# Second mixing in seven pieces of 64 keys instead of eight overlapping ones, and the next block's scores ranked ahead

## The chip, the cores and the metric

One core of one Trainium2 chip runs the whole program. Its engines are named as in the profile: PE is TensorE (matmul; PEld its weight loads), DVE VectorE, ACT ScalarE, POOL GpSimd, SP SyncE, which issues the transfers. The metric is the device time of one execution in microseconds (us); three timed runs give a median.

## The reference

```python
scores = scale * np.matmul(q, k.transpose(0, 1, 3, 2))       # 4 batches, 12 heads, 448 tokens, 64 wide
scores = np.einsum('bhij,hg->bgij', scores, w_pre)           # first mixing of the heads
scores = scores - np.max(scores, axis=-1, keepdims=True)
attn = np.exp(scores)
attn = attn / (np.sum(attn, axis=-1, keepdims=True) + 1e-09)
attn = np.einsum('bhij,hg->bgij', attn, w_post)              # second mixing
out = np.matmul(attn, v)
...
h = x @ w_in;  x = (h * np.cos(h)) @ w_out                   # 1792 tokens, 768 -> 2048 -> 768
h = np.maximum(np.maximum(x @ w1, x @ w2), x @ w3);  out = h @ w_out2
```

## The kernel before, in words

The first part of the program is attention, in float32; the rest are the two MLPs, whose products run as three matmuls of split operands (`three`, L155 to L159).

Attention goes by score blocks. `HALVES` cuts each batch's 448 rows into four blocks of 10, 12, 12 and 11 slots in some order; a slot is ten rows, as two groups `a` of five. There are 16 blocks, numbered 0 to 15 here, and 180 slots. One, or two neighbouring, blocks form a half (`halves`), ten in all, of m columns (100 to 230).

For each block and each pair of heads, `qk` (L546 to L554) makes scores of up to 120 rows by 448 keys in PSUM; there are six pairs, so six score products a block. `evac` copies each head's scores to SBUF, and `send` (L565 to L567) scatters them by DMA into a grid whose partitions are row times head, so that mixing over heads becomes a contraction over partitions. There are two grids; block n writes the one that block n - 2 used, and may do so when that block's last first mixing is done.

A visit takes two slots of a grid. `mix1` (L569 to L577) is the first mixing, `rowmax` and `soft` the maximum and the exponentials, `wscale` puts the reciprocal sums into the second mixing's weights. `mix2` (L607 to L618) is the second mixing: per slot and row group the exponentials of 64 keys are the weights, and 60 columns (five rows, twelve heads) stream. The 448 keys are four groups `j` of 112 (`JB, JC = 4, 112`), each as two pieces of 64 that overlap by 16, one in PSUM's partitions 0 to 63 and one in 64 to 127:

```python
o = j * JC + c * (JC - 64)
nc.tensor.matmul(live["a", v, y][64 * c:64 * c + 64, j, :, a, :], live["e", v, a][k, o:o + 64],
                 live["w2s", v][k, a], start=True, stop=True)
```

`keep` (L620 to L626) copies the 480 columns of a slot from PSUM into `a2`. The 16 rows that stand twice meet zero rows of the value tiles: `vget` (L534 to L538) loads 56 rows into partitions 0 to 55 and 56 into 72 to 127. When a half is kept, `av` (L632 to L641) multiplies it by the values, two head pairs at a time, three times a half: per pair four groups `j` by two heads, 128 partitions by m columns. `keepx` and `out` write the result to DRAM as xT.

PSUM has two banks for `mix2` and `av` together (`ps_t`), two for `qk` (`ps_x`) and four for `mix1` (`ps_m`).

The order of all engines' work is made by a planner (`Plan`, L373 to L442). Each step has a rank, a cost per engine, what it follows, the ring places it takes and the steps that free them. At each point the planner takes, of the steps that could start soon on an engine, the one of lowest rank, and advances its clock by the given cost; the instructions are then written in that order, and each engine takes its own in order. Ranks count half visits: visit y has rank 2y for `mix1`, 2y + 1.5 for `mix2`. The score products of block n have rank `first[n - 1] + 0.5 + 0.125 * slots * hp`, so they spread over the visits of block n - 1 (L684).

Near the end of attention the first weights of the MLP are loaded and split, x of the first batch is loaded (`xget`, L140) and cut into two parts (L144 on ACT, L148 on DVE or POOL), and the first hidden products (`hidden`, L157 to L159) stand between the last visits.

Of the kernel before, what the change touches and what calls it, by code (L numbers as in the profile page):

```python
# [9 lines left out]
F32 = mybir.dt.float32  # L10
# [12 lines left out]
JB, JC = 4, 112  # L23
# [421 lines left out]
def attention(ctx, tc, q, k, v, w_pre, w_post, same_row, xT, tp, mlps):  # L445
# [24 lines left out]
    places = [vp.tile([128, JB, 2, D], F32, name=f"v{x}") for x in range(BUFS["v"])]  # L470
# [11 lines left out]
    for b, sizes in enumerate(HALVES):  # L482
        i = 0
        for n, half in enumerate(sizes):
            start, column, nhalf = min(i, S - RI * half[0]), 0, len(halves)
            for slots in half:
                i = min(i, S - RI * slots)
                score.append((b, i, RI * slots, slots, nhalf, column))
                column += RI * slots
                i += RI * slots  # L490
            halves.append((b, start, i - start, column, range(len(score) - len(half), len(score))))
# [42 lines left out]
    def vget(b, hp, eng):  # L534
        live["v", b, hp] = places[(b * H // 2 + hp) % len(places)]
        for a in range(2):
            to, of = a * (128 - JC // 2), a * JC // 2
            queue_of[eng].dma_start(live["v", b, hp][to:to + JC // 2], v[b, hp][of:of + JC // 2])  # L538


    def score_bank(n, hp):
        grid = lambda: ps_t.tile([128, JB, H, RI], F32, name="aps").rearrange("p j g i -> p (j g i)")[:, :S]
# [76 lines left out]

    def keep(v, y, eng):  # L620
        n, t, _ = visits[v]
        half, o = score[n][4], score[n][5] + RI * (t + y)
        if ("a2", half) not in live:
            live["a2", half] = ap_.tile([128, JB, H, NHALF], F32, name="a2")
        copy(eng, live["a2", half][:, :, :, o:o + RI].rearrange("p j g i -> p (j g) i"),
             live["a", v, y][:].rearrange("p j g a r -> p (j g) (a r)"))  # L626
# [5 lines left out]
    def av(half, x, _):  # L632
        b, _, _, m, _ = halves[half]
        a2 = live["a2", half]
        both = ps_t.tile([128, JB * H * RI], F32, name="aps")
# [588 lines left out]
```

## Time and profile before

| what | value |
|---|---|
| timed runs | 1157.16, 1154.21, 1155.92 us; median 1155.92 |
| profiled execution | 1158.33 us, span 1156.5 us |
| granted TensorE clock, mean | 0.992 |
| PE busy | 1124.7 us (97%) |
| DVE, ACT, POOL busy | 979.4 (85%), 667.0 (58%), 76.0 us (7%) |
| longest groups on PE | L157, L158, L159: 300.5, 299.8 and 299.3 us and three more; L617 (`mix2`) 119.9 us |

The span is what the profiler saw from the first to the last instruction of one execution; the execution's own time lies 1.83 us above it. Attention takes up to about 376 us, the MLPs the rest. Busy times of one engine can overlap in themselves: matmuls are pipelined, and up to four small ones run beside each other in parts of the array, so the distance from one start to the next says more than a duration. The planner's costs are no measurement.

### The profile page before, as it was taken

Reading aid. Unit: us, or ns where it says so; the run is one execution under the profiler, and the core shown is the slowest. Engines: PE = TensorE matmul, PEld = TensorE weight load, DVE = VectorE, ACT = ScalarE, POOL = GpSimd, SP = SyncE. Lnnn points to the kernel's source line nnn. Section 1 sums busy time; section 2 is a strip of 40 time slices with the busy share of each in tenths; the row PEclk is TensorE's granted clock in tenths of the full one; section 3 lists DMA queues with packets and bytes.
Section 4 is the critical chain, followed back from the end, with each engine's and each line's share of the span. In section 5 each row is a group of like instructions: output and inputs, shape, how many; then the busy total and the mean of one; then the engine's idle time right before and its main releaser. Section 6 shows DMA issues by size and latency. Waiting matters only on the chain.

```text
span 1156.5 us, 29873 instructions
## 1 busy us (share of the span) xinstructions
PE 1124.7 (97%) x12028; PEld 944.2 (82%) x12028; DVE 979.4 (85%) x2057; ACT 667.0 (58%) x1497; POOL 76.0 (7%) x66
## 2 busy tenths in 40 slices
PE   7989999899999999999999999999999999999998
PEld 2667666666657899999999999999999999999987
DVE  5777777777878999999999999998887779778994
ACT  3767666566757776555555555655634454445572
POOL 4000000000004200000000000000001021011110
PEclk8999999999998999999999999999999999999999
DMA  7786665645454654344444444431012211222233
GB/s 228 214 220 191 188 199 160 190 146 155 150 165 123 217 153 147 122 124 121 126 130 124 126 127 122 131 109 35 1 35 83 73 50 35 82 62 69 82 119 114
DMA packets 92426, 146.05 MB, mean 126 GB/s; under 512 B 12192, under 2 KB 75264, under 8 KB 92288
## 3 DMA queue, kind: packets, MB, share of 16 engines
q1 hardware_dynamic: 92032, 144.13, 41.2%
q8 instruction: 94, 1.54, 0.6%
q14 instruction: 44, 0.36, 0.1%
q0 software_dynamic: 256, 0.02, 0.0%
HBM read 84.96 MB, written 20.45 MB: 91 GB/s over the span
## 4 chain that ended last, share of the span: by engine, by line
PE 88%; DVE 6%; DMA 3%; issue 2%; ACT 1%; SPq 0%; DVEq 0%; ACTq 0%
PE ps L157 21%; PE ps L159 21%; PE ps L158 21%; PE aps L617 7%; PE mps L576 6%; PE aps L640 6%; PE ps L553 5%; DVE nm L584 1%; DMA k<-in_k_dram 1%; DMA wraw<-in_w_in_dram 1%; DMA t<-s 1%; DVE xs L461 0%; DVE x L148 0%; DVE s L461 0%; DVE x L334 0%
## 5 line engine op out<-in xcount | busy, mean ns | idle before, releaser
L159 PE MATMUL ps<-x,w 128*128 128x448 f32 x816 | 299.8, 367 | 2.4 <-DVE x L148 1.7
L157 PE MATMUL ps<-x,w 128*128 128x448 f32 x816 | 300.5, 368 | 0.9 <-ACT gh L866 0.6
L158 PE MATMUL ps<-x,w 128*128 128x448 f32 x816 | 299.3, 367 | 0.3 <-DVE w L297 0.3
L159 PEld LDWEIGHTS ps<-x,w 128*128 128x128 f32 x816 | 153.4, 188 | 17.5 <-DVE x L148 3.0
L157 PEld LDWEIGHTS ps<-x,w 128*128 128x128 f32 x816 | 153.3, 188 | 16.5 <-ACT gh L866 1.0
L158 PEld LDWEIGHTS ps<-x,w 128*128 128x128 f32 x816 | 153.3, 188 | 13.8 <-DVE w L297 0.7
L617 PEld LDWEIGHTS aps<-w2s,e 60*64 60x64 f32 x5760 | 118.6, 136 | 48.0 <-issue 28.9
L157 PE MATMUL ps<-gh,w 128*128 128x448 f32 x384 | 140.9, 367 | 0.0
L158 PE MATMUL ps<-gh,w 128*128 128x448 f32 x384 | 140.7, 366 | 0.0
L159 PE MATMUL ps<-gl,w 128*128 128x448 f32 x384 | 140.4, 366 | 0.0
L617 PE MATMUL aps<-w2s,e 60*64 60x60 f32 x5760 | 119.9, 221 | 12.3 <-issue 8.0
L590 ACT ACTIVATE e<-mps,nm 128x448 f32<-128x448 f32 (+1 forms) x184 | 116.4, 645 | 14.0 <-DVE nm L584 11.8
L294 ACT CAST w<-wf 128x384 fp32r<-128x384 f32 x168 | 81.1, 514 | 73.7 <-DVE wf L286 55.1
L584 DVE TENSOR_REDUCE nm<-mps 128x1 f32<-128x448 f32 (+1 forms) x184 | 107.5, 616 | 17.1 <-PE mps L576 15.7
L553 PE MATMUL ps<-k,q 64*64 64x448 f32 (+3 forms) x736 | 101.7, 557 | 4.4 <-ACT s L461 2.0
L576 PE MATMUL mps<-t,w 64*64 64x448 f32 (+1 forms) x720 | 96.5, 562 | 4.6 <-DMA k<-in_k_dram 1.7
L823 DVE TENSOR_TENSOR acc<-ps,acc 128x448 f32<-128x448 f32 x168 | 100.3, 615 | 0.6 <-PE ps L159 0.6
L253 ACT ACTIVATE wf<-wraw 128x384 f32<-128x384 f32 x112 | 61.9, 553 | 56.4 <-DMA wraw<-in_w_out_dram 35.5
L297 DVE TENSOR_TENSOR w<-wf,w 128x384 fp32r<-128x384 f32 x132 | 74.6, 585 | 18.7 <-ACT w L294 17.9
L297 POOL TENSOR_TENSOR w<-wf,w 128x384 fp32r<-128x384 f32 x36 | 41.9, 1171 | 681.8 <-DVE wt L257 373.4
L640 PEld LDWEIGHTS aps<-a,v 128*64 128x64 f32 x960 | 58.8, 138 | 30.6 <-ACT a L461 11.5
L461 ACT COPY a<-aps 128x480 f32<-128x480 f32 x104 | 58.1, 574 | 44.0 <-PE aps L617 43.9
(121 smaller groups left out, 1764.3 us busy)
## 6 DMA issues: line engine op xcount, KB each, us to landing
t<-s SPq DMA_DIRECT2D x96, 210.0 KB
wf<-w SPq DMA_DIRECT2D x96, 192.0 KB
wraw<-in_w_out_dram SPq DMA_DIRECT2D x44, 384.0 KB
wraw<-in_w_dram SPq DMA_DIRECT2D x36, 384.0 KB
wraw<-in_w_in_dram SPq DMA_DIRECT2D x32, 384.0 KB
t<-s SPq DMA_DIRECT2D x48, 192.5 KB
w<-wf SPq DMA_DIRECT2D x48, 192.0 KB
t<-s SPq DMA_DIRECT2D x42, 175.0 KB
```

Of the source, the lines that this page charges most:

```text
L157: mm(w[0], x[0], start=first, stop=False)
L158: mm(w[1], x[0], start=False, stop=False)
L159: mm(w[0], x[1], start=False, stop=last)
L294: return nc.scalar.copy(A[x][0], w())
L297: return eng.tensor_sub(A[x][1], w(), f32(A[x][0]))
L553: nc.tensor.matmul(live["s", n, 2 * hp + g][r:end], live["q", b, hp][half, i0 + r:i0 + end], live["k", b, hp][half], start=True, stop=True)
L576: nc.tensor.matmul(live["m", v, a][64 * y:64 * y + 64], w1[k], grids[n % 2][k, t + y, :], start=True, stop=True)
L584: nc.vector.tensor_reduce(nm, of(v, live["m", v, a]), axis=AX.X, op=ALU.max, negate=True)
L590: nc.scalar.activation(of(v, e), of(v, live["m", v, a]), AF.Exp, bias=live["nm", v, a], scale=1.0, accum_out=live["z", v][:, a:a + 1])
L617: nc.tensor.matmul(live["a", v, y][64 * c:64 * c + 64, j, :, a, :], live["e", v, a][k, o:o + 64], live["w2s", v][k, a], start=True, stop=True)
L640: nc.tensor.matmul(ps[64 * g:64 * g + 64, :m], live["v", b, hp][:, j, g, :], a2[:, j, 2 * hp + g, :m], start=j == 0, stop=j == JB - 1)
L823: return nc.vector.tensor_add(acc, po, acc) if fg else nc.scalar.copy(acc, po)
```

## The change

The keys are now seven pieces of 64 (`JB, JC = 7, 64`). Pieces 0 to 2 go to partitions 0 to 63 and pieces 4 to 6 to partitions 64 to 127, each for both row groups; piece 3 goes to the low half for row group 0 and to the high half for row group 1. That makes 14 matmuls a slot for 16, and 7 x 60 = 420 columns in PSUM and in `a2`, whose layout becomes piece, head, row. `vget` loads 64 rows twice: partitions 0 to 63 get pieces 0 to 3, partitions 64 to 127 pieces 3 to 6, in a tile of five places whose corner halves stay zero. `av` runs three groups of full columns and two of half the columns, on weights whose other half is zero. `keepx` reads and writes in two halves of columns. Ranks: score products start three half visits earlier and lie closer; the planner counts 5.0 us for a send to land for 3.5, and less for `mix2` and `keep`.

```diff
-JB, JC = 4, 112
+JB, JC = 7, 64
+JP = JB // 2
...
-    places = [vp.tile([128, JB, 2, D], F32, name=f"v{x}") for x in range(BUFS["v"])]
+    places = [vp.tile([128, JP + 2, 2, D], F32, name=f"v{x}") for x in range(BUFS["v"])]
...
-            to, of = a * (128 - JC // 2), a * JC // 2
-            queue_of[eng].dma_start(live["v", b, hp][to:to + JC // 2], v[b, hp][of:of + JC // 2])
+            to = live["v", b, hp][JC * a:JC * a + JC, 1 - a:JP + 2 - a]
+            queue_of[eng].dma_start(to, v[b, hp][:, JP * a:JP * a + JP + 1])
...
-            live["a", v, y] = ps_t.tile([128, JB, H, RI], F32, name="aps").rearrange("p j g (a r) -> p j g a r", r=RH)
-        for j in range(JB):
-            for a in range(2):
-                for y in slots:
-                    k = slice(64 * y, 64 * y + PH)
-                    for c in range(2):
-                        o = j * JC + c * (JC - 64)
-                        nc.tensor.matmul(live["a", v, y][64 * c:64 * c + 64, j, :, a, :], live["e", v, a][k, o:o + 64],
-                                         live["w2s", v][k, a], start=True, stop=True)
+            live["a", v, y] = ps_t.tile([128, 512], F32, name="aps")[:, :JB * PH].rearrange("p (u m) -> p u m", m=PH)
+        parts = [(y, c, 2 * j + a, a, j + c * (JP + 1)) for j in range(JP) for a in range(2) for y in slots for c in range(2)]
+        for y, c, u, a, j in parts + [(y, a, 2 * JP, a, JP) for y in slots for a in range(2)]:
+            k = slice(64 * y, 64 * y + PH)
+            nc.tensor.matmul(live["a", v, y][64 * c:64 * c + 64, u], live["e", v, a][k, j * JC:j * JC + JC],
+                             live["w2s", v][k, a], start=True, stop=True)
...
-        copy(eng, live["a2", half][:, :, :, o:o + RI].rearrange("p j g i -> p (j g) i"),
-             live["a", v, y][:].rearrange("p j g a r -> p (j g) (a r)"))
+        copy(eng, live["a2", half][:, :, :, o:o + RH].rearrange("p u g r -> p (u g) r"),
+             live["a", v, y].rearrange("p u (g r) -> p (u g) r", r=RH))
...
-            ps = live["av", hp] = both[:, n * NHALF:(n + 1) * NHALF]
-            for j in range(JB):
+            ps = live["av", hp] = both[:, n * NHALF:n * NHALF + m].rearrange("p (a w) -> p a w", a=2)
+            for j in (*range(1, JP + 1), 0, JP + 1):
                 for g in range(2):
-                    nc.tensor.matmul(ps[64 * g:64 * g + 64, :m], live["v", b, hp][:, j, g, :], a2[:, j, 2 * hp + g, :m],
-                                     start=j == 0, stop=j == JB - 1)
+                    of = live["v", b, hp][:, j, g, :]
+                    to, rows = ps[64 * g:64 * g + 64], a2[:, :, 2 * hp + g, :w]
+                    if 0 < j <= JP:
+                        nc.tensor.matmul(to, of, rows[:, 2 * j - 2:2 * j], start=j == 1, stop=False)
+                    else:
+                        a = 0 if j else 1
+                        nc.tensor.matmul(to[:, a], of, rows[:, 2 * JP], start=False, stop=j > 0)
...
-            r = (first[n - 1] + 0.5 + 0.125 * score[n - 1][3] * hp) if n else -40.0 + hp
+            r = (first[n - 1] - 2.5 + 0.1 * score[n - 1][3] * hp) if n else -40.0 + hp
...
-        add(mix2, (y,), i + 1.5, {"T": 0.04 + 0.465 * len(slots)}, [key("wscale")], turn=True, takes=["ps_t"] * len(slots),
+        add(mix2, (y,), i + 1.5, {"T": 0.04 + 0.41 * len(slots)}, [key("wscale")], turn=True, takes=["ps_t"] * len(slots),
...
-            add(keep, (y, c), i + 1.5, {"A": 0.45, "V": 0.57}, [key("mix2")], turn=True, lands=0.17, takes=["a2"] * begin,
+            add(keep, (y, c), i + 1.5, {"A": 0.41, "V": 0.51}, [key("mix2")], turn=True, lands=0.17, takes=["a2"] * begin,
...
-            add(av, (half, x), r, {"T": 0.2 + 0.0139 * halves[half][3]}, [("vget", b, hp) for hp in pairs(x)] + ends, turn=True, takes=["ps_t"],
+            add(av, (half, x), r, {"T": 0.25 + 0.0139 * halves[half][3]}, [("vget", b, hp) for hp in pairs(x)] + ends, turn=True, takes=["ps_t"],
```

The rank moves instructions on every engine. In the rows below a line, the operation, out<-in and the shape of what streams; two rows of `qk` (L553 before, L554 now) are one score product, L576 and L577 are `mix1`, L617 and L615 `mix2`, L640 and the pair L641, L644 `av`; lines of the new kernel are one to four off.

TensorE, between the last score product of block 6 and the first mixing of block 6. Before, from that score product on:

```order
L553 MATMUL ps<-k,q 64x448 x2
L553 MATMUL ps<-k,q 56x448 x2
L576 MATMUL mps<-t,w_124 64x448 x4
L617 MATMUL aps<-w2s,e 64x12x5 x32
L576 MATMUL mps<-t,w_124 64x448 x4
L553 MATMUL ps<-k,q 64x448 x2
L553 MATMUL ps<-k,q 46x448 x2
L617 MATMUL aps<-w2s,e 64x12x5 x32
L553 MATMUL ps<-k,q 64x448 x2
L553 MATMUL ps<-k,q 46x448 x2
L617 MATMUL aps<-w2s,e 64x12x5 x32
L576 MATMUL mps<-t,w_124 64x448 x4
```

Now, where that score product and one second mixing stand directly ahead of the first row:

```order
L577 MATMUL mps<-t,w_124 64x448 x4
L554 MATMUL ps<-k,q 64x448 x2
L554 MATMUL ps<-k,q 46x448 x2
L615 MATMUL aps<-w2s,e 64x60 x28
L577 MATMUL mps<-t,w_124 64x448 x4
L554 MATMUL ps<-k,q 64x448 x2
L554 MATMUL ps<-k,q 46x448 x2
L615 MATMUL aps<-w2s,e 64x60 x28
L554 MATMUL ps<-k,q 64x448 x2
L554 MATMUL ps<-k,q 46x448 x2
L615 MATMUL aps<-w2s,e 64x60 x28
L577 MATMUL mps<-t,w_124 64x448 x4
```

The last row of each is the first mixing of block 6. Seven products lay between, now nine, and three score products of block 7 (46 rows in their second part) for two.

TensorE, at the last mixing of block 6, whose grid block 8 (36 rows in the second part) writes. Before, the mixing, a product with the values, then the first score product of block 8:

```order
L576 MATMUL mps<-t,w_124 64x448 x4
L640 MATMUL aps<-a_2185,v_127 64x220 x8
L640 MATMUL aps<-a_2185,v_128 64x220 x8
L553 MATMUL ps<-k,q 64x448 x2
L553 MATMUL ps<-k,q 36x448 x2
```

Now:

```order
L554 MATMUL ps<-k,q 64x448 x2
L554 MATMUL ps<-k,q 36x448 x2
L577 MATMUL mps<-t,w_124 64x448 x4
L641 MATMUL aps<-a_2114,v_127 64x220 x6
L644 MATMUL aps<-a_2114,v_127 64x110 x4
L641 MATMUL aps<-a_2114,v_128 64x220 x6
L644 MATMUL aps<-a_2114,v_128 64x110 x4
```

The score product went ahead of the mixing. Of blocks 2 to 15 this holds for twelve, before for three (5, 9 and 13).

TensorE, at the end of attention, from the third mixing of block 15 before, and from the second mixing ahead of it now (L157 to L159, now L158 to L160, are the first hidden products):

```order
L576 MATMUL mps<-t,w_124 64x448 x4
L617 MATMUL aps<-w2s,e 64x12x5 x32
L576 MATMUL mps<-t,w_124 64x448 x4
L617 MATMUL aps<-w2s,e 64x12x5 x32
L576 MATMUL mps<-t,w_124 64x448 x4
L640 MATMUL aps<-a_6536,v_130 64x120 x8
L640 MATMUL aps<-a_6536,v_131 64x120 x8
L640 MATMUL aps<-a_6536,v_132 64x120 x8
L640 MATMUL aps<-a_6536,v_126 64x120 x8
L157 MATMUL ps<-x,w 128x448
L158 MATMUL ps<-x,w 128x448
L159 MATMUL ps<-x,w 128x448
```

```order
L615 MATMUL aps<-w2s,e 64x60 x28
L158 MATMUL ps<-x,w 128x448
L159 MATMUL ps<-x,w 128x448
L160 MATMUL ps<-x,w 128x448
L577 MATMUL mps<-t,w_124 64x448 x4
L615 MATMUL aps<-w2s,e 64x60 x28
L577 MATMUL mps<-t,w_124 64x448 x4
L615 MATMUL aps<-w2s,e 64x60 x28
L577 MATMUL mps<-t,w_124 64x448 x4
L641 MATMUL aps<-a_6305,v_130 64x120 x6
L644 MATMUL aps<-a_6305,v_130 64x60 x4
```

The first hidden product stood behind the fifth mixing and two products with the values; now it stands ahead of the third mixing. From there on TensorE's instructions of the MLPs come in the same order as before.

## Rows read from the trace of the kernel before

**Rows 1.** The page's part 1: busy time, share of the span, instructions.

```profile
PE 1124.7 (97%) x12028; PEld 944.2 (82%) x12028; DVE 979.4 (85%) x2057; ACT 667.0 (58%) x1497; POOL 76.0 (7%) x66
```

**Rows 2.** Busy time by stretches: PE, PEld, DVE, ACT, POOL, granted clock, DMA share, GB/s.

```profile
23.00:352.00 329.00, 311.33 (x7738) 212.68 (x7732) 249.78 (x670) 216.94 (x594) 0.99 (x1) 0.99 0.60 179
352.00:376.00 24.00, 22.25 (x435) 18.11 (x432) 23.20 (x42) 18.64 (x43) 12.61 (x10) 0.93 0.40 123
376.00:1156.50 780.50, 774.07 (x3780) 708.61 (x3779) 694.30 (x1326) 424.06 (x848) 48.89 (x42) 1.00 0.33 101
```

**Rows 3.** The chain of waits from 23 to 376 us, shares by line.

```profile
by line: PE aps L617 22.9%; PE mps L576 18.2%; PE aps L640 18.1%; PE ps L553 14.9%; issue 4.9%; DVE nm L584 3.0%; DMA k<-in_k_dram 2.7%; DMA t<-s 1.9%; DVE xs L461 1.4%; DVE s L461 1.3%; ACT xs L461 1.3%; DVE wt L261 1.2%; ACT e L590 1.0%; 
```

**Rows 4.** Timeline of TensorE, steady visits: start, us, engine, line, operation.

```profile
183.66 0.96 PE L553 MATMUL ps<-k,q 64*64 64x448 f32 x8
184.41 1.14 PE L617 MATMUL aps<-w2s,e 60*64 60x60 f32 x64
185.34 0.97 PE L576 MATMUL mps<-t,w 64*64 64x448 f32 x8
```

**Rows 5.** Timeline of TensorE: products with the values, and what follows.

```profile
151.46 3.19 PE L640 MATMUL aps<-a,v 128*64 128x220 f32 x32
154.58 0.97 PE L553 MATMUL ps<-k,q 64*64 64x448 f32 x8
...
370.59 1.59 PE L640 MATMUL aps<-a,v 128*64 128x100 f32 x32 [0.23 <-DVE a L461]
372.11 0.47 PE L157 MATMUL ps<-x,w 128*128 128x448 f32 x1
```

**Rows 6.** Groups by line over the whole span: busy us, mean ns.

```profile
L617 PE MATMUL aps<-w2s,e 60*64 60x60 f32 x5760 | 119.9, 221 | 12.3 <-issue 8.0 <-DVE xs L461 2.7 <-ACT xs L461 0.9
...
L461 ACT COPY a<-aps 128x480 f32<-128x480 f32 x104 | 58.1, 574 | 44.0 <-PE aps L617 43.9
L461 DVE COPY s<-ps 120x448 f32<-120x448 f32 (+2 forms) x95 | 57.6, 618 | 7.7 <-PE ps L553 5.7 <-DMA t<-s 0.3
...
L461 DVE COPY a<-aps 128x480 f32<-128x480 f32 x76 | 49.6, 652 | 18.4 <-PE aps L617 18.4
```

**Rows 7.** Waits from 23 to 376 us: in total, times, longest.

```profile
PEld aps L640 <- ACT a L461: 11.5, 15, 1.4
...
PE aps L617 <- issue: 8.0, 5, 2.4
...
PEld aps L617 <- ACT a L461: 6.3, 12, 0.7
...
PE mps L576 <- DMA k<-in_k_dram: 1.7, 1, 1.7
...
PE mps L576 <- DMA t<-s: 1.0, 1, 1.0
...
PE mps L576 <- DMA q<-in_q_dram: 0.5, 1, 0.5
```

**Rows 8.** Timeline, last score product and first mixing of block 3.

```profile
72.13 0.97 PE L553 MATMUL ps<-k,q 64*64 64x448 f32 x8
...
80.88 0.98 PE L576 MATMUL mps<-t,w 64*64 64x448 f32 x8 [1.66 <-DMA k<-in_k_dram]
```

**Rows 9.** Timeline at the end of attention, all engines.

```profile
336.09 0.98 PE L576 MATMUL mps<-t,w 64*64 64x448 f32 x8
...
336.64 0.82 SPq L655 DMA_DIRECT2D xT<-xs  x2
...
338.05 0.39 SPq L140 DMA_DIRECT2D x<-xT  x1
...
348.95 1.06 DVE L148 TENSOR_TENSOR x<-x 128x448 fp32r<-128x448 f32 x1 [1.98 <-ACT x L144]
...
357.02 0.74 PE L159 MATMUL ps<-x,w 128*128 128x448 f32 x1 [0.66 <-DVE x L148]
```

**Rows 10.** Waits of SyncE's queue from 23 to 376 us.

```profile
SPq L567 <- PE mps L576: 5.4, 3, 2.2
```

More of the change, by code (lines that the diff above doesn't have):

```diff
@@ L488, in attention @@
                 score.append((b, i, RI * slots, slots, nhalf, column))
-                column += RI * slots
+                column += RH * slots
                 i += RI * slots
-            halves.append((b, start, i - start, column, range(len(score) - len(half), len(score))))
+            halves.append((b, start, i - start, 2 * column, range(len(score) - len(half), len(score))))
     visits = [(n, t, range(min(2, x[3] - t))) for n, x in enumerate(score) for t in range(0, x[3], 2)]
@@ L536, in vget @@
         for a in range(2):
-            to, of = a * (128 - JC // 2), a * JC // 2
-            queue_of[eng].dma_start(live["v", b, hp][to:to + JC // 2], v[b, hp][of:of + JC // 2])
+            to = live["v", b, hp][JC * a:JC * a + JC, 1 - a:JP + 2 - a]
+            queue_of[eng].dma_start(to, v[b, hp][:, JP * a:JP * a + JP + 1])
     def score_bank(n, hp):
-        grid = lambda: ps_t.tile([128, JB, H, RI], F32, name="aps").rearrange("p j g i -> p (j g i)")[:, :S]
+        grid = lambda: ps_t.tile([128, 512], F32, name="aps")[:, :S]
         return (("ps", lambda: ps_x.tile([128, S], F32, name="ps")), ("ps_t", grid),
@@ L609, in mix2 @@
         for y in slots:
[L610 to L618 removed]
+            live["a", v, y] = ps_t.tile([128, 512], F32, name="aps")[:, :JB * PH].rearrange("p (u m) -> p u m", m=PH)
[4 more added lines that the diff above has]
+                             live["w2s", v][k, a], start=True, stop=True)
     def keep(v, y, eng):
         n, t, _ = visits[v]
[L622 removed]
+        half, o = score[n][4], score[n][5] + RH * (t + y)
         if ("a2", half) not in live:
[L624 to L626 removed]
+            live["a2", half] = ap_.tile([128, JB, H, NHALF // 2], F32, name="a2")
+        copy(eng, live["a2", half][:, :, :, o:o + RH].rearrange("p u g r -> p (u g) r"),
+             live["a", v, y].rearrange("p u (g r) -> p (u g) r", r=RH))
     def pairs(x):
@@ L633, in av @@
         b, _, _, m, _ = halves[half]
-        a2 = live["a2", half]
-        both = ps_t.tile([128, JB * H * RI], F32, name="aps")
+        a2, w = live["a2", half], m // 2
+        both = ps_t.tile([128, 512], F32, name="aps")
         for n, hp in enumerate(pairs(x)):
-            ps = live["av", hp] = both[:, n * NHALF:(n + 1) * NHALF]
-            for j in range(JB):
+            ps = live["av", hp] = both[:, n * NHALF:n * NHALF + m].rearrange("p (a w) -> p a w", a=2)
+            for j in (*range(1, JP + 1), 0, JP + 1):
                 for g in range(2):
-                    nc.tensor.matmul(ps[64 * g:64 * g + 64, :m], live["v", b, hp][:, j, g, :], a2[:, j, 2 * hp + g, :m],
-                                     start=j == 0, stop=j == JB - 1)
+                    of = live["v", b, hp][:, j, g, :]
[5 more added lines that the diff above has]
+                        nc.tensor.matmul(to[:, a], of, rows[:, 2 * JP], start=False, stop=j > 0)
     def keepx(half, hp, eng):
@@ L649, in keepx @@
             o = i0 - halves[half][1]
-            copy(eng, xs[:, o:o + m].rearrange("p (r t) -> p r t", t=slots),
-                 ps[:, c:c + m].rearrange("p (t r) -> p r t", r=RI))
+            copy(eng, xs[:, o:o + m].rearrange("p (a r t) -> p a r t", a=2, t=slots),
+                 ps[:, :, c:c + m // 2].rearrange("p a (t r) -> p a r t", r=RH))
     def out(half, hp, eng):
@@ L695, in attention @@
                     plan.add(("new_t", n), r, lambda _: None, {}, [("evac", n, 0)], takes=["t"])
-                add(send, (n, h), r, {"D": score[n][2] / 125.0}, [("evac", n, h), ("new_t", n)], turn=True, frees=[(place, ("evac", n, h))], lands=3.5)
+                add(send, (n, h), r, {"D": score[n][2] / 125.0}, [("evac", n, h), ("new_t", n)], turn=True, frees=[(place, ("evac", n, h))], lands=5.0)
     for y, (n, t, slots) in enumerate(visits):
```

## The prediction

> **What bounds the kernel now.** I read the page first, then the busy time by stretches, then the chain of waits over attention, then single stretches of TensorE. Over the span TensorE is busy 97% [rows 1]. By stretches [rows 2]: from 376 us on, where the two MLPs run, TensorE idles 780.5 - 774.07 = 6.4 us in 780; nothing there is touched by the change, and its TensorE instructions stand in the same order. What can move is attention, from 23 to 376 us. TensorE idles 329 - 311.33 = 17.7 us in its first 329 and 1.8 us in its last 24. The chain over this stretch [rows 3] lies on TensorE's four products for 74% of the time, the second mixing alone 22.9%; 4.9% is TensorE waiting for nothing the profile shows, 4.6% the loads of k and the sends of scores into the grid. So a pass taken from TensorE should shorten attention nearly one to one, and the MLPs follow when attention ends.
>
> The profiled execution took 1158.33 us, 2.4 above the median 1155.92 and above all three timed runs. The terms are taken from it; I subtract their sum from the median.
>
> **1. Second mixing, 16 to 14 matmuls a slot.** The trace has two records (passes) for each matmul: 180 slots x 16 x 2 = 5760 [rows 6]. After it are 5040, 720 fewer. In a steady visit 64 passes start at 184.41 and the next product at 185.34 [rows 4]: 0.93 us, 14.5 ns a pass, although one pass alone lasts 221 ns [rows 6], since passes overlap. 720 x 14.5 ns = **-10.4 us**. From another view: 22.9% of the 353 us is 80.8, an eighth of it 10.1. Bounds: visits behind a product with the values wait for its copies first, and one visit in each block boundary waits for its own exponentials; 30 + 16 of 92 visits could swallow their share, which leaves half, -5.3. On the other side I allow -11.5, one microsecond of the stalls in the midst of this product (term 4) that may go with its passes.
>
> **2. Product with the values, 8 to 10 matmuls a head pair.** Columns stay the same (4m before; 3m and two halves after), passes go from 30 products x 16 x 2 = 960 to 1200. 32 passes of 220 columns take 154.58 - 151.46 = 3.12 us, 32 of 100 columns 372.11 - 370.59 = 1.52 us [rows 5]: 0.417 ns a column and 5.8 ns that do not depend on columns. 240 x 5.8 = **+1.4 us**. Lower bound 0 (both halves of the array overlap the extra start); upper bound: no pass takes less than the shortest of this form shown, 47.5 ns. Then the 96 passes of 60 columns cost 16.7 ns more each and the 96 of 50 columns 20.8 ns: +3.6, in all +5.0. I take 1.4, since the line through both rows is what this kind of pass does. The Trainium skill, page "TensorEngine Tiling (Array Packing)", section Performance Considerations, says that each matmul carries some 60 cycles of overhead; as an estimate from that page, 25 ns for each added pass at 2.4 GHz, the term would be +6.0 and the sum below -7.2. By that rule a pass of the second mixing could not cost 14.5 ns either, so on packed tiles the trace does not agree.
>
> **3. Copies of the second mixing, 480 to 420 columns.** VectorE takes 652 ns at 480 and 618 at 448 columns [rows 6]: 1.1 ns a column, 64 ns less a copy; ScalarE, 574 at 480, can save no more than an eighth, 72. I take 64 on both: 180 copies, 11.5 us of busy time on two engines. That lies beside TensorE's work: it pays only where a weight load waits for such a copy, in 12 + 15 waits on ScalarE [rows 7]. 27 x 64 ns = 1.7, of which I take half, since the engine may still run earlier passes while the next load waits: **-0.8 us**, bounds 0 and -1.7. Should the runs of five columns where ten lay together slow the copies, the gain is 0; ScalarE, busy 216.94 of 329 us [rows 2], has the room.
>
> **4. Scores of the next block earlier.** Before a block's first mixing the last of its twelve sends must land. At block 3 the last score product starts at 72.13 and the mixing only at 80.88, with TensorE idle 1.66 us [rows 8]. Three first mixings waited so, 1.7 + 1.0 + 0.5 = 3.2 us [rows 7], at blocks 3, 2 and 6. In the old order 4 to 7 products, 6.0 in the mean, lie between a block's last score product and its first mixing; in the new one 7 to 10, mean 8.9 (the pieces under the change show 7 and 9). Three more products of 0.75 (183.66 to 184.41) to 0.93 us [rows 4] are over 2.2 us, more than the longest of the waits, so all three should go. Smaller waits around the boundaries, on exponentials and copies where mixings bunch, should shrink too: **-4.0 us**. Bounds: 0, if another transfer is late instead; and all of TensorE's idle time but the stalls on nothing shown, 17.7 - 8.0 [rows 2, 7], which is -9.7. I stay close to the waits that have a name. The 8.0 us, five stalls of up to 2.4 us in the midst of the second mixing, I leave as they are.
>
> **5. First hidden product moved ahead.** The new order puts the first three matmuls of the first MLP before the third mixing of the last block; it stood behind the fifth. TensorE takes its matmuls in order, so if their operands are late, this mixing waits, and behind it the last visits' maxima, exponentials and products. Operands: the load of x stands on SyncE's queue behind the output of the last product with the values of the half before it (336.64), and went out at 338.05; its first piece was cut on VectorE by 348.95 + 1.06 = 350.0 [rows 9], 13.9 us after that product ended (336.09, where the next mixing starts). In the new order x stands behind the output of the second such product, and from that one's end to the first hidden matmul TensorE has one product with the values, three mixings and four second mixings, about 3.3 + 2.2 + 3.3 = 8.8 us. So it can stand 5.1 us. Against that, the load itself starts earlier, and the hidden products that waited for cut pieces before (0.66 us at 357.02 [rows 9]) find them done. I take **+2.0 us**, bounds 0 and +5.1.
>
> **At nothing:** values loaded in 64 rows for 56, 24 pairs of loads on SyncE as before, hidden under the transfers' 60% share [rows 2]; longer clears of the value tiles at the start, under the first loads; the strided halves in the output copies, same columns.
>
> **Sum:** -10.4 + 1.4 - 0.8 - 4.0 + 2.0 = -11.8, from the median **1144.1 us**. Its own range, with terms 1 to 5 not all at one end, is 1137 to 1150.
>
> **The rivals.**
> *A. The order gives nothing.* Waits at the boundaries come back as others (loads of q and k behind the earlier sends), and the hidden product stands its full 5.1 us: -10.4 + 1.4 - 0.8 + 0 + 5.1 = -4.7, 1151.2 us. For it: transfers are 60% busy and the sends share one queue; against it: three whole products of slack. 0.19.
> *B. Short passes cost a floor.* Term 2 is +5.0: -8.2, 1147.7 us. The Trainium skill, page "TensorEngine Tiling (Array Packing)", section Performance Considerations, points this way. For it: no row shows a pass of this form under 47.5 ns; against it: the second mixing's rows start one each 14.5 ns. 0.07.
> *C. Slower: SyncE's queue blocks.* A block's sends need the grid that the block two before leaves with its last mixing. In the old order the first score product stands ahead of that mixing at 3 blocks, and the sends waited on the first mixing exactly 3 times, 5.4 us [rows 10], 1.8 each; in the new order it stands ahead at 12. Behind a waiting send lie loads of q, k and values and the outputs; score products wait for those. If 9 more waits of 1.8 us came through, +16.2 and no gain in term 4: -7.8 + 16.2 = +8.4, 1164.3 us. It decides from (7.8 + 3.5) / 9 = 1.3 us a boundary on. Against it: the three old cases lie at blocks 5, 9 and 13, and none of these is among the three first mixings that waited for a landing [rows 7], so the queue took 1.8 us without passing it on. 0.07.
> *D. No measurable change.* The passes saved lie under waits (term 1 at -5.3), term 2 is +1.4, term 5 +5.1 and nothing else comes: +1.2, 1157.1 us. The chain on TensorE speaks against it. 0.08.
>
> **How the numbers follow.** The forecast has 0.59. A measurement of this kernel tells 0.3%, 3.5 us, from no change. Forecast, A and B are faster by more, 0.85; D with the near edge of C is within, 0.09; slower 0.06. For 8 in 10 the range takes in the forecast's own, B and A's time, and below it 2 us of term 4 towards its bound: 1135 to 1152.
>
> **What would show it.** Right: second mixing 5040 records and its steady visit near 0.81 us; values 1200 records with the 100-column product near 1.57 us; no wait for a landing before a first mixing; attention ending near 364 us for 376, and the MLP stretch still 780 us. Wrong: the MLP stretch longer (the saved time waits for weights); SyncE's sends waiting on TensorE for over 15 us with score products idle behind them; a TensorE wait over 5 us at the first hidden product; visits still 0.93 us long.

## The result, and the profile after

The changed kernel took **1143.42 us** in the median of four runs (1142.08 to 1143.54); the kernel before, beside it, 1156.54 (1154.21 to 1157.92). The ratio is 0.9895 with a 95% interval of 0.9872 to 0.9917. The forecast was 1144.1 us. The sum came out; two of its five terms did not, and their errors cancelled, which is luck. The profiled execution took 1143.35 us, its span is 1141.5.

The page's first part, to be laid beside [rows 1], and the steady visits and products with the values, beside [rows 4, 5] (start, us, engine, line, operation):

```profile
PE 1112.7 (97%) x11548; PEld 936.5 (82%) x11548; DVE 974.8 (85%) x2060; ACT 661.9 (58%) x1493; POOL 76.7 (7%) x67
```

```profile
183.68 1.02 PE L615 MATMUL aps<-w2s,e 60*64 60x60 f32 x56
184.50 0.97 PE L577 MATMUL mps<-t,w 64*64 64x448 f32 x8
...
44.76 0.76 PE L641 MATMUL aps<-a,v 128*64 128x100 f32 x12
...
46.41 0.98 PE L554 MATMUL ps<-k,q 64*64 64x448 f32 x8
...
147.55 1.36 PE L641 MATMUL aps<-a,v 128*64 128x220 f32 x12
...
150.71 0.59 PE L554 MATMUL ps<-k,q 64*64 64x448 f32 x4
```

TensorE has 480 records less: 720 fewer in the second mixing, 240 more in the product with the values. A steady second mixing lasts from 183.68 to 184.50, 0.82 us for 0.93. A product with the values of 100 columns takes 46.41 - 44.76 = 1.65 us for 1.52, one of 220 columns 3.16 for 3.12.

The stretches, the cuts of [rows 2] moved to where attention now begins and ends (PE, PEld, DVE, ACT, POOL, granted clock, DMA share, GB/s):

```profile
24.00:340.00 316.00, 301.92 (x7241) 205.99 (x7243) 249.66 (x681) 212.03 (x589) 3.86 (x4) 0.98 0.65 189
340.00:363.00 23.00, 20.12 (x449) 17.22 (x444) 20.87 (x36) 17.05 (x40) 11.00 (x10) 1.00 0.49 143
363.00:1141.50 778.50, 773.52 (x3784) 708.88 (x3781) 692.53 (x1325) 424.40 (x851) 48.33 (x40) 1.00 0.34 101
```

Attention ends at 363 us for 376. The MLPs take 778.5 us for 780.5, where the forecast had them at 780 still. From the first mixing to that end TensorE still idles 339 - 322.04 = 17.0 us, for 353 - 333.58 = 19.4 before [rows 2]: the time came off its busy time, 322.0 us for 333.6. The chain from 24 to 363 us says the same: the second mixing holds 19.5% of it for 22.9% [rows 3], and the sends 6.0% for 1.9%.

```profile
by line: PE aps L615 19.5%; PE mps L577 18.8%; PE ps L554 15.3%; PE aps L641 12.3%; DMA t<-s 6.0%; PE aps L644 4.0%; issue 3.7%; DMA x<-xT 2.5%; ACT e L591 2.3%; DMA xT<-xs 1.9%; DVE nm L585 1.5%; DVE xs L462 1.5%; ACT xs L462 1.2%; DVE wt 
```

What it idles on did change (waits from 24 to 363 us: total, times, longest; beside [rows 7]):

```profile
PE mps L577 <- DMA xT<-xs: 4.6, 2, 2.7
...
PE aps L615 <- DVE a L462: 2.0, 3, 0.8
PE aps L615 <- ACT xs L462: 1.5, 1, 1.5
PE aps L615 <- ACT a L462: 1.3, 3, 0.6
PE aps L615 <- issue: 1.2, 2, 0.7
...
PE mps L577 <- DMA t<-s: 0.8, 1, 0.8
```

The stalls on nothing shown, inside the second mixing, fell from 8.0 us to 1.2. The landing waits before first mixings did not go: 0.8 + 4.6 = 5.4 us for 3.2 before. (Second profiles of the two kernels, below, have 4.5 and 7.0, so that the amount alone tells little.) The longest is again at block 3, and it costs more than itself (timeline of TensorE):

```profile
82.08 1.77 PE L577 MATMUL mps<-t,w 64*64 64x448 f32 x8 [2.74 <-DMA xT<-xs]
83.63 1.71 PE L615 MATMUL aps<-w2s,e 60*64 60x60 f32 x56
85.12 1.72 PE L554 MATMUL ps<-k,q 64*64 64x448 f32 x8
86.62 1.66 PE L577 MATMUL mps<-t,w 64*64 64x448 f32 x8
88.11 0.98 PE L615 MATMUL aps<-w2s,e 60*64 60x60 f32 x56
```

The wait is put down to a store of an output, which came last by the profile; the mixing itself waits for its block's sends. Behind the 2.74 us, four products take 6.03 us (82.08 to the start of the next second mixing, 88.11) where a steady second mixing (0.82) and three steady products (0.75 each, [rows 4]) need 3.07. The windows around them (columns as above):

```profile
82.08:88.90 6.82, 6.82 (x136) 3.79 (x140) 3.18 (x8) 2.32 (x6) 0.00 (x0) 0.56 0.79 217
88.90:95.00 6.10, 6.10 (x148) 3.81 (x140) 5.68 (x18) 5.05 (x14) 0.00 (x0) 1.00 0.85 220
```

The granted clock is 0.56 in the first, near the lower of its two levels (1.2 of 2.4 GHz), and 1.00 in the second. TensorE had stood idle ahead of the fall. This wait cost 2.7 + 3.0 us.

### The profile page after: what moved, and what is told of

It reads as the page before. It is cut to its first block, busy times and chain, and to the rows that moved or that the text cites. A ratio compares the mean times of both kernels' runs of the same rounds, so it can differ in the third digit from the quotient of the medians.

```text
span 1141.5 us, 28936 instructions
## 1 busy us (share of the span) xinstructions
PE 1112.7 (97%) x11548; PEld 936.5 (82%) x11548; DVE 974.8 (85%) x2060; ACT 661.9 (58%) x1493; POOL 76.7 (7%) x67
## 4 chain that ended last, share of the span: by engine, by line
PE 86%; DMA 5%; DVE 4%; ACT 2%; issue 1%; SPq 1%; POOL 0%; ACTq 0%; DVEq 0%; POOLq 0%
PE ps L158 22%; PE ps L159 22%; PE ps L160 22%; PE aps L615 6%; PE mps L577 6%; PE ps L554 5%; PE aps L641 4%; DMA t<-s 2%; DMA x<-xT 1%; PE aps L644 1%; DMA k<-in_k_dram 1%; ACT e L591 1%; DMA xT<-xs 1%; DMA t<-e 1%; DVE nm L585 0%
## 5 line engine op out<-in xcount | busy, mean ns | idle before, releaser
L158 PE MATMUL ps<-x,w 128*128 128x448 f32 x816 | 300.0, 368 | 0.8 <-ACT gh L869 0.6
L160 PE MATMUL ps<-x,w 128*128 128x448 f32 x816 | 299.1, 367 | 0.3
L159 PE MATMUL ps<-x,w 128*128 128x448 f32 x816 | 299.1, 367 | 0.3 <-DVE w L298 0.3
L158 PEld LDWEIGHTS ps<-x,w 128*128 128x128 f32 x816 | 153.2, 188 | 15.3 <-ACT gh L869 1.0
L160 PEld LDWEIGHTS ps<-x,w 128*128 128x128 f32 x816 | 153.2, 188 | 14.9 <-POOL x L149 1.0
L159 PEld LDWEIGHTS ps<-x,w 128*128 128x128 f32 x816 | 153.2, 188 | 14.0 <-DVE w L298 0.7
L615 PEld LDWEIGHTS aps<-w2s,e 60*64 60x64 f32 x5040 | 103.7, 136 | 49.6 <-issue 25.9
L158 PE MATMUL ps<-gh,w 128*128 128x448 f32 x384 | 140.8, 367 | 0.0
L159 PE MATMUL ps<-gh,w 128*128 128x448 f32 x384 | 140.7, 366 | 0.0
L160 PE MATMUL ps<-gl,w 128*128 128x448 f32 x384 | 140.4, 366 | 0.0
L615 PE MATMUL aps<-w2s,e 60*64 60x60 f32 x5040 | 105.4, 220 | 8.9 <-DVE xs L462 2.4
L554 PE MATMUL ps<-k,q 64*64 64x448 f32 (+3 forms) x736 | 101.0, 561 | 2.9 <-ACT s L462 2.7
L577 PE MATMUL mps<-t,w 64*64 64x448 f32 (+1 forms) x720 | 95.8, 567 | 7.3 <-DMA xT<-xs 4.6
L160 PEld LDWEIGHTS ps<-gl,w 128*128 128x128 f32 x384 | 72.1, 188 | 6.5
L158 PEld LDWEIGHTS ps<-gh,w 128*128 128x128 f32 x384 | 72.1, 188 | 6.3
```

The lines of the kernel that those rows point to most:

```text
L158: mm(w[0], x[0], start=first, stop=False)
L159: mm(w[1], x[0], start=False, stop=False)
L160: mm(w[0], x[1], start=False, stop=last)
L554: nc.tensor.matmul(live["s", n, 2 * hp + g][r:end], live["q", b, hp][half, i0 + r:i0 + end], live["k", b, hp][half], start=True, stop=True)
L577: nc.tensor.matmul(live["m", v, a][64 * y:64 * y + 64], w1[k], grids[n % 2][k, t + y, :], start=True, stop=True)
L615: nc.tensor.matmul(live["a", v, y][64 * c:64 * c + 64, u], live["e", v, a][k, j * JC:j * JC + JC], live["w2s", v][k, a], start=True, stop= ...
```

## The experiments

Two readings stood after this. **P**: the passes make the gain, and order gives nothing. **O**: the earlier scores bring what the passes don't. It was also open whether the stalls inside the second mixing hang on its number of matmuls, or are chance. All runs are compared with the kernel before on the same chip; its median was 1156.3 in the first group (24 runs), 1155.4 in the second (11), 1156.1 in the third (23).

### Order and pieces apart

`order_alone`, the kernel before with two numbers of the change:

```diff
-r = (first[n - 1] + 0.5 + 0.125 * score[n - 1][3] * hp) if n else -40.0 + hp
+r = (first[n - 1] - 2.5 + 0.1 * score[n - 1][3] * hp) if n else -40.0 + hp
-... add(send, ...) lands=3.5
+... add(send, ...) lands=5.0
```

> The kernel before with two numbers of the change only: the scores' rank three places earlier and their landing time 5.0; the second mixing keeps its 16 matmuls a slot. Theory P: no gain, 1156 to 1158 us, since the landing waits only move to other blocks (5.3 us in the changed kernel, 3.2 before). Theory O: 1152.5 to 1153.5. A third reading (the earlier scores crowd SyncE's queue, and the passes hid it) would make it slower, 1159 or more.

Measured: 1157.55 us, ratio 1.0024 (0.9994 to 1.0053). No gain, as P says; reading O falls for the old kernel. A landing wait moved, too: the longest, 3.3 us, is at block 4 now.

`pieces_alone`, the changed kernel with this diff turned round:

> The changed kernel (seven pieces, ten matmuls with the values) with the old order: the old rank of the next block's scores and the old landing time of 3.5. Theory P (passes): the whole difference of 13.1 us hangs on the 720 passes saved, -10.4 us of TensorE, and on stalls inside the second mixing that went with them; then the time is 1143 to 1145 us. Theory O (order): the passes give -10.4 + 1.6 - 0.8 = -9.6 and the earlier scores the other 3.5; then it is near 1147. By both the second mixing's steady visit is 0.81 us and the second mixing has 5040 records; by O the landing waits of 3.2 us before first mixings are there and instruction stalls stay near 8 us, by P the stalls are below 3 us.

Measured: **1164.44 us, ratio 1.0080 (1.0052 to 1.0108)**. Neither reading had this: half of the change makes the kernel slower than it was, though the second mixing has its 5040 records. What this run still held of the change besides the pieces were the planner's costs (second mixing 0.41 a slot for 0.465, copies 0.41/0.51 for 0.45/0.57, values 0.25 for 0.2). Two more runs fill the table. `pieces_old_numbers` sets the three costs back too:

```diff
-add(mix2, (y,), i + 1.5, {"T": 0.04 + 0.41 * len(slots)}, ...
+add(mix2, (y,), i + 1.5, {"T": 0.04 + 0.465 * len(slots)}, ...
-add(keep, (y, c), i + 1.5, {"A": 0.41, "V": 0.51}, ...
+add(keep, (y, c), i + 1.5, {"A": 0.45, "V": 0.57}, ...
-add(av, (half, x), r, {"T": 0.25 + 0.0139 * halves[half][3]}, ...
+add(av, (half, x), r, {"T": 0.2 + 0.0139 * halves[half][3]}, ...
```

> The changed kernel with all of the planner's old numbers: rank, landing time, and the old costs of second mixing, copies and product with the values (0.465, 0.45/0.57, 0.2). TensorE's products then stand in exactly the order of the kernel before, with 14 matmuls for 16 and 10 for 8. Theory R (the run with new costs and old rank lost because that pairing of numbers bunches the mixings): the pieces alone are worth -10.4 + 1.6 - 0.8 = -9.6, so 1146 to 1148 us. Theory S (the pieces shorten the second mixing, so that any order made for the longer one leaves boundary waits): 1152 or more. If the instruction stalls hang on the passes, up to 4 us below R, 1143.

> The changed kernel, unaltered, timed beside the others on the same chip; its last single time there was 1147.4. By R the order of the change gives only what the pieces already give, so it stands within 3 us of the kernel with the old numbers; by S it is 5 us or more below it. Time 1143 to 1147.

`new_rank_old_costs` is the changed kernel with these three costs set back:

> The pieces, the new rank and the landing time of 5.0, with the old costs of second mixing, copies and product with the values: the fourth corner beside the changed kernel (1143.2), old rank with old costs (1146.7) and old rank with new costs (1164.4). In the order it gives, two first mixings stand directly one behind the other once, in the change 5 times, in old rank with old costs 7 times, in old rank with new costs 19 times. If the bunching of mixings is what costs, it is no slower than the change: 1140 to 1144. If the new costs were needed because they are nearer to what the pieces take, it loses: 1148 or more.

All four have the seven pieces, the same matmuls and the same copies; only the order differs. Median, and ratio to before with its interval:

| | old costs | new costs |
|---|---|---|
| old rank | 1146.74, 0.9921 (0.9900 to 0.9941) | 1164.44, 1.0080 (1.0052 to 1.0108) |
| new rank | 1150.25, 0.9953 (0.9928 to 0.9977) | 1143.20, 0.9902 (0.9881 to 0.9924) |

In the order of the kernel before, product for product, the pieces give 0.79%, 9.1 us, with an uncertainty of 2.4: reading R of the expectation. The profiles agree: from 22 to 365 us TensorE is busy 323.86 us and idle 19.1, where it was busy 333.58 and idle 19.4 before. The change's order adds 0.19%, 2.2 us, with an uncertainty of some 3.5 us from both intervals, so that it can't be told from nothing. But the new costs with the old rank lose 18 us against that order, and the old costs with the new rank some 4, at the edge of its uncertainty; against the change these lose 6. Rank and costs are one setting, not two terms.

Of the 17.5 us between the two profiles 357 - 343 = 14 lie in attention, the rest behind it. Where the 14 lie is seen in the waits of the weight loads, which stand under passes that are still running and so hardly show as idle time of TensorE. First `pieces_alone` from 22 to 379 us, then `pieces_old_numbers` from 22 to 365 (total, times, longest):

```profile
PEld aps L615 <- ACT a L462: 11.2, 28, 0.8
PEld mps L577 <- ACT e L591: 9.9, 24, 0.8
...
PEld ps L554 <- ACT s L462: 7.6, 19, 1.4
```

```profile
PEld aps L615 <- ACT a L462: 9.0, 18, 1.5
...
PEld mps L577 <- ACT e L591: 4.0, 13, 0.8
```

First mixings wait 24 times for exponentials, for 13, and score products 19 times for copies of scores. In this order two first mixings stand directly one behind the other 19 times, for 7 in the old one; as I read it, the second of them then wants banks that still wait for exponentials. By the windows TensorE idles 357 - 333.78 = 23.2 us here, and 343 - 323.86 = 19.1 in the other; its busy time is 9.9 us more for the same matmuls. The count of such pairs is not the whole rule, though: `new_rank_old_costs` has one pair, the change five, and it is the slower of the two. By attention alone the guess is neither shown nor gone: from the first mixing to the last product with the values it is 343 us at one pair, 339 to 344 in three profiles at five, 343 at seven and 357.5 at nineteen. Which feature of an order sets its cost stays open.

Part of it lies outside attention. From the last product with the values to the end, with the same matmuls in every kernel, the profiles have 778.3 to 778.9 us in the change and 780.3 in the old order with the pieces, but 782.1 in `new_rank_old_costs`, 783.5 in `pieces_alone` and 784.0 in `order_alone`. In `new_rank_old_costs` the first mixing also starts at 26.0 us for 22.0 in the old order, and attention itself is as long as there; whether that start belongs to the order or to the one execution is not shown.

### The price of the passes

`spare_passes` gives back the passes and leaves the order:

```diff
-... + [(y, a, 2 * JP, a, JP) for y in slots for a in range(2)]:
+... + [(y, a, 2 * JP, a, JP) for y in slots for a in range(2)] + [(y, c, 2 * j + 1, 1, j + c * (JP + 1)) for y in slots for j in (2,) for c in range(2)]:
```

> The changed kernel with two more matmuls a slot in the second mixing, which write one piece a second time with the same values: 16 a slot as before, 5760 records, with the order, the copies and the product with the values of the change. Theory P with every pass at 14.5 ns: 720 x 14.5 = +10.4 us against the changed kernel, so 1153.8, and the steady visit back at 0.93 us; if stalls inside the second mixing hang on the number of passes, up to 4 us more, 1157. Theory O: the passes were partly hidden by waits, and the extra ones cost 6 us or less, 1149.5 or below.

Measured: 1152.48 us, ratio 0.9975 (0.9950 to 1.0001). Against the change that is 0.73%, 8.4 us, with an uncertainty of 3.9. Its steady visit:

```profile
164.14 1.14 PE L615 MATMUL aps<-w2s,e 60*64 60x60 f32 x64
165.07 0.96 PE L554 MATMUL ps<-k,q 64*64 64x448 f32 x8
```

0.93 us, as before the change. That agrees with 14.5 ns a pass (10.4 us); 6 us or less, which O wanted, is not excluded.

### Are the stalls chance?

> The changed kernel again, unaltered, for a second profile. If the instruction stalls (1.2 us in the first profile, 8.0 before) and the landing waits (0.8 at block 1, 2.7 at block 3, 1.8 at block 7) belong to the program, they come back at the same visits with the same lengths within 0.5 us; if they are chance of one execution, the stalls turn up elsewhere, by several us more or less. Time 1142 to 1144 by either.

> The kernel before, unaltered, for a second profile. If stalls of TensorE inside the second mixing on nothing the profile shows belong to 16 matmuls a slot, it has 5 to 10 us of them again (8.0 in the first profile; 4.8 and 6.7 in the two other kernels with 16 a slot, 1.2 to 4.2 in the seven with 14); if they are chance, it may as well have 2.

Times 1147.43 and 1161.74 us, one execution each; the first lies outside the 1142 to 1144 that were expected. The views are TensorE's waits, of which the lines on `issue` are the stalls on nothing shown, inside the second mixing; first `before_again` (23 to 378 us), then `after_again`:

```profile
PE aps L617 <- issue: 6.1, 7, 2.1
PE mps L576 <- DMA xT<-xs: 5.9, 2, 3.9
```

```profile
PE mps L577 <- ACT e L591: 3.3, 2, 2.8
PE mps L577 <- DMA k<-in_k_dram: 3.2, 1, 3.2
...
PE aps L615 <- issue: 1.5, 3, 0.9
```

In part they stand at one place of the program: both profiles of the kernel before have one at the same record of TensorE's order, 1.92 us at 149.5 and 0.82 at 152.0, and another, 2.26 us at 346.1 and 2.07 at 348.1; the rest fall elsewhere each time. The four profiles with 16 matmuls a slot have 8.0, 6.1, 5.7 and 3.1 us of them, the ten with 14 at most 2.6, in the mean about 1. With the stalls inside other products, which the expectation counted too, it is 9.4, 6.9, 6.5 and 4.6 us against 4.0 at most. So there are more with the 16, though one execution differs from the next by some 2 us.

What TensorE lacks there can be read from the transfers. In the kernel before (transfers from 23 to 376 us: queue, kind, packets, MB, share; and one of the stalls):

```profile
q8 instruction: 65, 1.06, 1.3%
```

```profile
226.66 0.44 PE L617 MATMUL aps<-w2s,e 60*64 60x60 f32 x10 [2.38 <-issue]
```

This queue brings packets of 16,384 bytes, 94 of them over the span for TensorE's 12028 records, 91 for 11548, 96 for the 12268 of `spare_passes`: one for about 127 records, and as many weight loads. Ahead of the stall shown, such a packet moves from 223.87 to 225.11 us, and TensorE goes on 1.55 us behind its end. In the fourteen profiles TensorE has 54 stalls on nothing shown in attention; 52 of them end 1.25 to 1.66 us behind the end of such a packet, and they stand about 127 records, or a multiple of that, apart. So TensorE waits there for its own instructions. That is read from the traces alone; no run moved these packets. Why there are more with 16 is not shown: as an estimate from the steady visits, 127 records last 3.9 us with 16 (80 records in 2.43 us) and 4.1 with 14 (72 in 2.32), which leaves a packet more time.

Landing waits come back at block 3 in both kernels (2.0 us at 82.8 us in `before_again`, which has one of 3.9 us at block 2 besides), with lengths that vary by over a microsecond, and other waits move by as much.

### What the landing waits wait for

At block 3 the sends share SyncE's queue with the loads of the next batch (changed kernel; SPq is the issuing queue):

```profile
69.06 0.49 SPq L533 DMA_DIRECT2D q<-in_q_dram  x1
69.61 0.42 SPq L529 DMA_DIRECT2D k<-in_k_dram  x1
70.13 1.63 SPq L533 DMA_DIRECT2D q<-in_q_dram  x1
71.81 0.43 SPq L529 DMA_DIRECT2D k<-in_k_dram  x1
72.34 1.65 SPq L568 DMA_DIRECT2D t<-s  x2
74.08 0.46 SPq L533 DMA_DIRECT2D q<-in_q_dram  x1
74.65 1.63 SPq L568 DMA_DIRECT2D t<-s  x2
```

The last two sends belong to block 3's last score product, which starts here:

```profile
68.49 0.56 PE L554 MATMUL ps<-k,q 64*64 64x448 f32 x2
```

In the kernel before it starts at 72.13 [rows 8], and its sends go out here:

```profile
73.72 1.64 SPq L567 DMA_DIRECT2D t<-s  x2
```

They left 1.6 us behind their product; now they leave 6.2 us behind it, with five loads and two sends between. From there to the first mixing it is 7.2 us before (80.88) and 7.4 now (82.08). So the score product moved up, 13.6 us ahead of its first mixing for 8.8, and the queue took it back. The second profiles agree: 2.2 us from product to sends in `before_again`, 5.3 and 5.5 in the two others of the change.

In the program the rank of these loads is the scores' rank less `early`, so the change moved loads and sends up together. `no_later_loads` takes the loads of three batches away:

```diff
-queue_of[eng].dma_start(live["k", b, hp], k[b, hp])
+if b:
+    nc.gpsimd.memset(live["k", b, hp], 0.0)
+else:
+    queue_of[eng].dma_start(live["k", b, hp], k[b, hp])
```

and the same for q. The scores of these batches are zero then: this kernel leaves their attention out.

> The changed kernel without the loads of q and k of batches 1 to 3: GpSimd fills these 36 tiles with zeros in their place, so the scores of these batches are zero; TensorE's order and all other work stay. It takes 8.3 MB off the transfers of attention. If the landing waits of 5 to 9 us before first mixings (and the clock's fall behind them) come from sends that share the transfers with these loads, they fall below 2 us, and 5 to 8 us come off: 1135 to 1138. If the sends are late by themselves (their own length, their place in SyncE's queue, stores of the outputs), the waits stay within 2 us: 1141 to 1143.

Measured: 1135.86 us, ratio 0.9832 (0.9799 to 0.9865), 0.70% or 8.1 us below the change, with an uncertainty of some 4.5; the two profiles differ by 5.0 us over the stretch below. From 42 us on, behind block 1, no first mixing waits for a landing, and the granted clock is 1.00 for 0.99; first `no_later_loads`, then `after_timed`, over the same part of attention:

```profile
42.00:357.00 315.00, 305.52 (x7373) 216.67 (x7365) 258.19 (x682) 217.64 (x598) 28.22 (x43) 1.00 0.54 162
```

```profile
42.00:362.00 320.00, 306.01 (x7309) 217.29 (x7301) 255.51 (x679) 216.20 (x594) 14.83 (x13) 0.99 0.63 184
```

Block 3's last sends leave 2.3 us behind their product (68.94 and 71.20 us), and its first mixing waits no more. So the loads were what the later landing waits waited for. Whether by their places in SyncE's queue or by their bytes this run doesn't tell, since it takes away both, and it computes on zeros besides. Can the gain be had without taking the loads away? `loads_later` and `loads_earlier` change one number, `early = 8.0 if b else 20.0`, to 5.0 and to 14.0:

> The changed kernel with one number: the loads of the next batch's q and k three places later (5 for 8). TensorE's order stays; only SyncE's queue changes. In the profile of the change the sends of block 3 share the transfers with these twelve loads (72 to 77 us), and its first mixing waits 2.7 us. If the loads are what makes the sends late, the landing waits at blocks 3, 7 and 11 go and 3 to 6 us come off: 1139 to 1141. If the transfers are late as a whole, the wait moves to the score products, which then wait for q and k by as much: no change, or slower by up to 5 us.

> The same number the other way: the loads of q and k six places earlier (14 for 8). They then go out before most sends of block 3, as far as the ten places of k and nine of q are free. If the loads crowd the sends, the landing waits at blocks 3, 7 and 11 shrink too, 2 to 4 us off, 1140 to 1142; if the places hold the loads back and the queue waits behind them, the sends of block 2 or 3 start later and it is slower by 2 to 6 us.

Measured: 1146.28 us, 0.9930 (0.9907 to 0.9952), and 1144.14, 0.9910 (0.9888 to 0.9932). Neither helps. In the profile with later loads the first mixing of block 3 waits 1.1 us, but block 4's waits 3.7 (total, times, longest):

```profile
PE mps L577 <- DMA t<-s: 7.1, 3, 3.7
```

As I read it, the transfers are late as a whole, and moving them moves the wait. `rank_three` sets the scores' rank to `- 3.0 + 0.08 * ...`:

> The changed kernel with the scores' rank at 3.0 ahead and 0.08 a slot for 2.5 and 0.1; the order differs in the first batch and in the last visits alone, with mixings directly behind one another 3 times for 5. If earlier scores still gained at blocks 1 to 3, the landing waits there (0.8 and 2.7 us in the change) shrink: 1140 to 1142. If the sends' transfers limit them, no difference: 1142 to 1145.

Measured: 1151.34 us, 0.9964 (0.9941 to 0.9987), slower than the change and outside what either theory expected. Its profile has landing waits of 2.4, 2.3 and 0.6 us and one of 3.9 us for the copies of a product with the values near the end (347 us); about 4 of the 7 us lie behind attention, where the MLPs take 782.7 us for 778.3 to 778.9. Why a change of order in the first batch and the last visits costs this much was not settled. No version that computes everything beat the change.

## Why the prediction was right, term by term

**1 to 3, the pieces (-10.4 + 1.4 - 0.8 = -9.8): right.** The kernel with these alone, in the old order, is 9.1 us faster, with an uncertainty of 2.4. The visit fell by 0.11 us where 0.12 was forecast. (The lower bound, half of 10.4, is 5.2 and not 5.3.) *Term 2:* the products with the values grew by 0.13 us at 100 columns and 0.04 at 220; with 0.06 at 120 and 0.02 at 230 (6, 6, 6 and 12 products) that is 1.6 us. That is 6.7 ns for each of the 240 passes. By the Trainium skill, page "TensorEngine Tiling (Array Packing)", section Performance Considerations, each matmul carries some 60 cycles of overhead, by which, as an estimate, the term would be +6.0; these packed tiles don't show it. With 1.6 where it had 5.0, rival B falls. *Term 3* was right on VectorE (652 to 589 ns) and too large on ScalarE (574 to 563, where 64 were taken off); what it is worth in time no run shows by itself:

```profile
L462 DVE COPY a<-aps 128x420 f32<-128x420 f32 x86 | 50.7, 589 | 10.1 <-PE aps L615 10.0
L462 ACT COPY a<-aps 128x420 f32<-128x420 f32 x94 | 52.7, 563 | 37.2 <-PE aps L615 35.4
```

**4, scores earlier (-4.0): the step failed.** It said that three more products ahead of a first mixing outlast the longest landing wait, so all three waits go. That holds the landing fixed while the products move. But the loads of q and k are ranked from the scores, came earlier with them, and the faster TensorE asks for the same bytes in less time: DMA share 0.65 in attention for 0.60. At block 3 the product stood 13.6 us ahead of its mixing for 8.8, but its sends left 6.2 us behind it for 1.6. The waits stayed, 5.4 us, and with the clock's fall one of them cost twice its length. The other half of the step, that left the 8.0 us of stalls as they are, failed in the other direction: they fell by some 5 us, and did so in the old order with the pieces as well (2.6 us there). TensorE's idle time moved little in all, 19.4 to 17.0, and the term is worth -1 to -2 us: from the first mixing to the last product with the values it is 339, 344 and 341 us in the three profiles of the change, 343 in the old order with the pieces. That is within what one execution differs from the next.

**5, the first hidden product (+2.0, 0 to +5.1): wrong sign.** Its step said that the first hidden product can stand until x is loaded and cut, up to 5.1 us. It did not wait:

```profile
330.53 1.04 PE L615 MATMUL aps<-w2s,e 60*64 60x60 f32 x56 [0.54 <-ACT a L462]
331.50 0.47 PE L158 MATMUL ps<-x,w 128*128 128x448 f32 x1
```

The load was hardly late: ScalarE waits 0.5 us for it at 329.45, and the copy behind that cut is what the second mixing above waits for. And with x loaded 17 us earlier (320.82 us for 338.05, [rows 9]), some 4 of them when counted from the end of attention, its pieces are cut in time for the products after attention. The stretch of the MLPs is 778.5 us here and in `after_timed`, but 780.1 in `pieces_old_numbers`, where TensorE waits for such pieces between 375 and 400 us:

```profile
PE ps L160 <- DVE x L149: 1.0, 1, 1.0
PE ps L160 <- POOL x L149: 0.6, 1, 0.6
```

The same list of the changed kernel is empty. The term had named this gain and weighed it too low; the 5.1 us of standing were what it had wrong, and with them "the MLP stretch still 780 us", which gained 2. Terms 4 and 5 together were to give -2.0 and gave -2.2 by the ratios, with an uncertainty of some 3.5 and for other reasons: that they agree is luck.

**The rivals.** A was right on the landing waits and wrong on the hidden product. C fell: SyncE's sends wait on first mixings 1.8 us in all, in three waits as before [rows 10], where the waits were to be twelve:

```profile
SPq L568 <- PE mps L577: 1.8, 3, 0.7
```

D fell: the passes saved did not lie under waits, since the pieces alone give 9.1 us. That half of the change, the pieces with the new costs in the old rank, makes the kernel slower by 8 us or more is a rival which the prediction lacked.

## What to carry to other kernels

Where a planner makes the order, a new cost and a new rank are one change: price the pieces in the old order, and take the order as a term with both signs until the four corners are run. A slack in products hides a transfer only if the transfer does not move with the products; look in the program for what else is ranked from the thing you move, and in the trace for what stands ahead of the transfer in its queue. When an engine gets faster, add up all of its idle time before and after, since waits by name replace one another.

## What was not expected of the hardware

- Stalls of TensorE on nothing the profile's waits show, up to 2.6 us long, end 1.25 to 1.66 us behind the end of a 16,384-byte packet of its instructions in 52 of 54 cases, and stand multiples of about 127 matmul records apart. Inside the second mixing they are 3.1 to 8.0 us in four profiles at 16 matmuls a slot, at most 2.6 in ten at 14.
- A wait of 2.74 us was followed by 6.8 us at a granted clock of 0.56, in which four products took 6.03 us instead of 3.07: the wait's price doubled.
- Transfers of 8.3 MB less, at a DMA share of 0.54 for 0.63, gave 8 us (uncertain by 4.5), though TensorE is the engine that is busy 97% of the span.
- The copy of 420 columns for 480, in runs of five for ten, saved VectorE 63 ns and ScalarE 11.
